# Order of the k, q and V loads and casts in an attention and SwiGLU kernel

## The chip, the cores and the metric

The kernel runs on one core of one Trainium2 chip. The metric is the device time of one execution in microseconds. The mean granted TensorE clock counts half clock only after full clock has come for the first time: the 0.991 of the kernel before is its 6.83 us of half clock from 76.9 us on in 401.1 us, without the first 12.0 us. The engines are called TensorE, VectorE, ScalarE, GpSimd and SyncE; in profile lines they are PE (PEld for its weight loads), DVE, ACT, POOL and SP. A "q" behind a name is the engine's instruction queue.

## The reference, cut to what matters

```python
# 8 batches x 8 heads, 576 positions, head size 64
scores = 0.125 * q @ k.T + minimum(bias, 0)      # bias from a cumulative sum of max(s, 0)
scores[causal] = -1e9                            # above the diagonal
attn = softmax(scores)
x = (attn @ v)        # heads side by side: 4608 x 512
out = (silu(x @ w_gate) * (x @ w_val)) @ w_out   # 512 -> 1536 -> 512
```

## The kernel before

The program works on half-batches of four heads (16 of them). Heads 0 to 7 (batch 0) come first. After that the feed-forward stage of one block of 512 rows is interleaved with the attention of the next batch: a generator yields items of feed-forward work, and another yields pieces of attention. What this Python emits first for an engine comes first in that engine's timeline: in the kernel before V 1 had landed by 55.0 us, but its casts on GpSimd, emitted behind those of k, q 4, began at 59.57.

The k, q of a half-batch ("k, q 3" are those of half-batch 3, "V 1" is the V of batch 1) take this way: a load to SBUF in fp32, a cast to bf16, and a transposition. For half-batches 0 to 4 TensorE transposes them; from 5 on they go through a scratch in DRAM and are transposed by a DMA on the way back. V is loaded per batch in five pieces into one buffer, and from batch 1 on each piece is cast on GpSimd.

```python
raw = ctx.enter_context(tc.tile_pool(name="raw", bufs=3))        # k, q: three buffers each
...
loaded["v", b] = raw.tile([128, NCH, H, D], FP32, tag="rawv", bufs=1, name="rawv")   # V: one buffer
...
# first batch, h = head 0..7
if h == 3:
    aug(2, SP4)          # four small DMAs of bias rows, issued by SyncE
    load_qk(3)
if h == 7:
    aug(3, SP4)
    load_v(1, range(5))
    load_qk(4)
    cast_one(2, "k", nc.gpsimd)
    cast_one(2, "q", nc.gpsimd)
    w_load("o", 0)
    w_load("o", 1)
...
# attention from head 8 on: kk is the head, h the half-batch, step the head in it
if step == 3 and h + 2 < NPE:            # NPE = 5; only h = 2: casts of half-batch 4
    cast_one(h + 2, "k", nc.gpsimd)
    cast_one(h + 2, "q", nc.gpsimd)
...
for ci in range(4):
    score_piece(kk, ci)                  # matmuls, exp on ScalarE, causal mask on GpSimd
    if ci == 1:
        side(h, step)                    # loads and casts ahead; casts of V 1 at head 11
...
PREP_AT = {                              # where TensorE transposes half-batch h + 1
    2: {(1, 3): 0, (2, 1): 1, (2, 3): 2, (3, 1): 3},
    3: {(0, 3): 0, (1, 3): 1, (2, 1): 2, (2, 3): 3},
}
...
hook = {                                 # at the n-th item of the first feed-forward block
    ...
    9: [lambda: cast_one(3, "k", nc.gpsimd), lambda: cast_one(3, "q", nc.gpsimd)],
    21: [lambda: load_qk(5)],
}
```

In `side`, the load of k, q `h + 3` is issued at the first head of half-batch h, from h = 3 on (so half-batch 6 at head 12), and V 2 is loaded at heads 10 and 11.

The softmax here doesn't subtract the row's maximum and nothing guards it: scores larger than these inputs give would overflow.

Of the kernel before, what the change touches and what calls it, by code (L numbers as in the profile page):

```python
# [19 lines left out]
def kernel(  # L20
# [11 lines left out]
    nc = tc.nc  # L32
# [48 lines left out]
    NPE = 5  # L81
# [24 lines left out]
    with tc.manual_schedule():  # L106
# [41 lines left out]
        def load_one(hb, name, rs=(0, NR)):  # L148
            b, g = divmod(hb, 2)
            if rs[0] == 0:  # L150
                loaded[name, hb] = raw.tile([128, NR, J, D], FP32, tag="raw" + name, name="raw" + name)
            nc.sync.dma_start(  # L152
                loaded[name, hb][:, rs[0] : rs[1], :, :].rearrange("x r j d -> x r (j d)"),
                SRC[name][0][b, g * HB + 2 * rs[0] : g * HB + 2 * rs[1], :, :].rearrange(
                    "(r e) (p j) d -> (e p) r (j d)", e=2, j=J
                ),
            )

        def load_qk(hb):
            load_one(hb, "k")  # L160
            load_one(hb, "q")

        def load_v(b, cs):
            if 0 in cs:
                loaded["v", b] = raw.tile([128, NCH, H, D], FP32, tag="rawv", bufs=1, name="rawv")
            t = loaded["v", b]
            for c in cs:
                n = 128 if c < 4 else TAIL
                nc.sync.dma_start(  # L169
                    t[0:n, c, :, :],  # L170
                    v[b, :, c * 128 : c * 128 + n, :].rearrange("h p d -> p h d"),
                )
# [12 lines left out]
        def aug(hb, engs):  # L185
            for hh in range(HB):
                r, e = divmod(hh, 2)
                r0 = 64 * (1 - r)
                bh = hb * HB + hh
                engs[hh].dma_start(  # L190
                    KQ[hb % 2][r][r0 : r0 + 4, :, e * S : (e + 1) * S],
                    HL[bh : bh + 1, :, :, :],
                )
# [48 lines left out]
        def cast_one(hb, name, eng):  # L242
            cts[name, hb] = cp.tile([128, J, NR, D], BF16, tag="c" + name, bufs=2, name="c" + name)
            dst = cts[name, hb].rearrange("x j r d -> x r j d")
            src_t = loaded[name, hb]
            if eng is nc.scalar:
                nc.scalar.copy(dst, src_t)
            else:
                eng.tensor_copy(dst, src_t)  # L249
# [75 lines left out]
        def w_load(kind, j, h=None):  # L325
            dst = {"g": WG, "v": WV, "o": WO}[kind][j]
            if kind == "o":
                src_ap = moe_w_out[j * WKO * 128 : (j + 1) * WKO * 128, :].rearrange(
                    "(c p) n -> p c n", p=128
                )  # L330
            else:
                w = moe_w_gate if kind == "g" else moe_w_val
                lo, hi = (0, WCH) if h is None else (h * WCH // 2, (h + 1) * WCH // 2)
                src_ap = w[:, j * WCH + lo : j * WCH + hi].rearrange("(c p) n -> p c n", p=128)
                dst = dst[:, :, lo:hi]
            nc.gpsimd.dma_start(dst, src_ap)
# [101 lines left out]
        def x_out(pr):  # L438
            nc.sync.dma_start(
                XS[pr].rearrange("(c p) d -> p c d", p=128), ots.pop(pr)  # L440
            )
# [6 lines left out]
        def x_pe(pr, eng=None):  # L448
            b, r = divmod(pr, H // 2)
            ot = ots.pop(pr)  # L450
            bs = take()
            ps = view16(bs, S)
            for c in range(NCH):
                n = 128 if c < 4 else TAIL
                nc.tensor.transpose(
                    ps[:, c * 128 : c * 128 + n], ot[0:n, c, :], ident[0:n, 0:n]
                )
            for lo, hi, at in x_parts(b):
                if eng is nc.scalar:
                    nc.scalar.copy(XT[:, r, at : at + hi - lo], ps[:, lo:hi])  # L460
                else:
                    nc.vector.tensor_copy(XT[:, r, at : at + hi - lo], ps[:, lo:hi])
            give(bs)
# [40 lines left out]
        def prep_one(hb, i):  # L504
            g, nm = divmod(i, 2)
            nm = ("k", "q")[nm]
            pe_transpose(hb, nm, g)
            for r in range(2):
                pe_out(hb, nm, g, r, nc.scalar if nm == "k" else nc.vector)

        PREP_AT = {
            2: {(1, 3): 0, (2, 1): 1, (2, 3): 2, (3, 1): 3},
            3: {(0, 3): 0, (1, 3): 1, (2, 1): 2, (2, 3): 3},
        }

        AV_AT = {
# [5 lines left out]
        def attn_items():  # L522
            for kk in range(H, BH + 2):
                h, step = divmod(kk, HB)
                if kk < BH:
                    if step == 3 and h + 2 < NPE:
                        cast_one(h + 2, "k", nc.gpsimd)
                        cast_one(h + 2, "q", nc.gpsimd)
                    if step == 0 and 3 < h + 1 < NPE:
                        aug(h + 1, GP4)  # L530
                    for ci in range(4):
                        score_piece(kk, ci)
                        if ci == 1:
                            side(h, step)
                        yield kk + 0.1 + ci / 8
                        if (step, ci) in PREP_AT.get(h, ()):
                            prep_one(h + 1, PREP_AT[h][step, ci])
                            yield kk + 0.1 + ci / 8
                for x in X_AT.get(kk, (kk - 2,)):
                    if x % 2 == 1 and H <= x < BH:  # L540
                        if x < XB * H:
                            x_pe(x // 2)
                            yield kk + 0.5
                        else:
                            x_in(x // 2)
                for p in AV_AT.get(kk, (kk - 1,)):
                    if H <= p < BH:
                        av_piece(p, (0, 1, 2))
                        yield kk + 0.6
                        av_piece(p, (3,))  # L550
                        yield kk + 0.7
                        av_piece(p, (4,))
                        av_out(p)
                        if p >= XB * H and p % 2 == 1:
                            x_out(p // 2)
                        yield kk + 0.8
# [103 lines left out]
        def first_batch():  # L660
            wq = {1: (("g", 0), ("v", 0)), 4: (("g", 1),), 5: (("v", 1),)}
            tail = {
                6: ("a0", "a1"),
                7: ("a2", "a3", "a4", "x0", "a5", "x1", "a6", "a7", "x2", "w6", "x3", "w8"),
            }
            for h in range(H):
                for ci in range(4):
                    score_piece(h, ci)
                for w in wq.get(h, ()):
                    w_load(*w)  # L670
                if h == 1:
                    order = [(nm, g) for g in range(2) for nm in ("k", "q")]
                    for nm, g in order:
                        pe_transpose(1, nm, g)
                    for r in range(2):
                        for nm, g in order:
                            pe_out(1, nm, g, r, nc.vector)
                    for c in range(3, 5):
                        cast_v(0, c, nc.vector)
                if h == 2:  # L680
                    for c in range(3):
                        cast_v(0, c, nc.gpsimd)
                if h == 3:
                    aug(2, SP4)
                    load_qk(3)
                if h == 7:
                    aug(3, SP4)
                    load_v(1, range(5))
                    load_qk(4)
                    cast_one(2, "k", nc.gpsimd)  # L690
                    cast_one(2, "q", nc.gpsimd)
                    w_load("o", 0)
                    w_load("o", 1)
                for what in tail.get(h, ()):
                    i = int(what[1:])
                    if what[0] == "a":
                        av_piece(i, range(NCH))
                        av_out(i)
                    elif what[0] == "x":
                        x_pe(i, nc.scalar)  # L700
                    else:
                        keep_warm(i)
# [6 lines left out]
        def pump(upto):  # L709
# [9 lines left out]
            2: [lambda: prep_one(2, 1)],  # L719
            3: [lambda: prep_one(2, 2)],  # L720
            4: [lambda: prep_one(2, 3)],
            9: [lambda: cast_one(3, "k", nc.gpsimd), lambda: cast_one(3, "q", nc.gpsimd)],
            21: [lambda: load_qk(5)],
        }
        for tt in range(NTT):
            lo = H * (tt + 1) + LAGS[tt]
# [40 lines left out]
```

## Time and profile before

| | kernel before |
|---|---|
| time, median of 4 | 403.07 us (401.6 to 405.39) |
| span of the profiled run | 401.1 us, mean clock 0.991 |
| TensorE busy | 370.0 us (92%) |
| idle of TensorE in gaps over 0.6 us, 30 to 380 us | 2.52 + 2.11 + 1.98 + 4.18 + 1.63 us |
| half clock | until 12.0 us, and 76.9 to 83.7 us |

The page has these two rows, with 40 slices of 10 us each. The first is the share of a slice in which TensorE was busy, in tenths, and the second the clock that it was granted, in tenths of full speed.

```profile
PE   3687959599999899999999999999999999999996
...
PEclk9999999889999999999999999999999999999999
```

From the ninth slice on TensorE is full, but for one 8 and the end. The two 8s of the clock row are the eighth and the ninth slice.

### The profile page before, as it was taken

The page shows a single profiled execution, that of the slowest core. Times are in us where ns is not written, and L with a number is a line of the kernel's source. Part 1 is how long each engine was busy: PE and PEld are TensorE (multiplying, and loading weights), DVE is VectorE, ACT ScalarE, POOL GpSimd, SP SyncE. Part 2 cuts the span into 40 slices and gives each one's busy share as a digit, 9 for nine tenths or more (in the row PEclk, how much of TensorE's full clock was granted, in tenths as well). Part 3 has the DMA queues.
Part 4 walks back from the last instruction along what each step waited for, and adds up shares of the span by engine and source line. Part 5 has one row for each costly group of instructions (what it writes and reads, how often), then busy time and mean ns, then how long its engine had stood idle before and what let it go on. Part 6 is the DMA issues. An engine that isn't in the chain of part 4 may idle for free.

```text
span 401.1 us, 7862 instructions
## 1 busy us (share of the span) xinstructions
PE 370.0 (92%) x2943; PEld 205.5 (51%) x2994; DVE 236.4 (59%) x431; ACT 214.1 (53%) x411; POOL 149.6 (37%) x270
## 2 busy tenths in 40 slices
PE   3687959599999899999999999999999999999996
PEld 3574535355555455555555555555555554444442
DVE  7865766316782287627952785479527743752750
ACT  7874963346665365555655565556556532323321
POOL 7780436454646173536453645364411100000000
PEclk9999999889999999999999999999999999999999
DMA  7999975693977697999688958794441014002002
GB/s 249 206 278 209 198 192 126 263 281 97 233 176 205 158 290 184 232 231 261 138 199 209 244 126 218 186 234 129 96 131 24 20 27 136 2 26 78 2 0 105
DMA packets 116982, 64.18 MB, mean 160 GB/s; under 512 B 97248, under 2 KB 101184, under 8 KB 116944
## 3 DMA queue, kind: packets, MB, share of 16 engines
q1 hardware_dynamic: 111456, 58.34, 57.1%
q0 software_dynamic: 5344, 5.21, 7.4%
q8 instruction: 23, 0.38, 0.4%
q10 hardware_dynamic: 144, 0.13, 0.1%
q14 instruction: 15, 0.12, 0.1%
HBM read 37.90 MB, written 19.86 MB: 144 GB/s over the span
## 4 chain that ended last, share of the span: by engine, by line
PE 76%; SPq 8%; DMA 7%; ACT 3%; DVE 2%; POOL 2%; issue 1%; POOLq 0%; ACTq 0%; DVEq 0%
PE bank L599 22%; PE bank L571 19%; PE bank L586 19%; PE bank L367 8%; SPq L169 7%; PE bank L405 6%; DMA rawk<-in_k_dram 2%; DMA pk<-ks 2%; DMA out_dram<-ysb 2%; PE wide L367 2%; ACT pt L380 1%; DMA rawq<-in_q_dram 1%; POOL vt L176 1%; SPq L152 1%; DVE ot L422 1%
## 5 line engine op out<-in xcount | busy, mean ns | idle before, releaser
L380 ACT ACTIVATE pt<-bank 128x512 bf16<-128x512 f32 x224 | 104.4, 506 | 49.1 <-PE bank L367 38.1
L578 DVE SCALAR_TENSOR_TENSOR pp<-th,bank 128x512 bf16<-128x512 bf16 x108 | 74.2, 687 | 80.4 <-ACT th L576 79.7
L586 PE MATMUL bank<-XT,wv 128*128 128x512 bf16 x421 | 109.4, 380 | 3.0 <-DMA wv<-in_moe_w_val_dram 2.5
L571 PE MATMUL bank<-XT,wg 128*128 128x512 bf16 x409 | 109.6, 380 | 1.7 <-DVE pp L578 0.2
L576 ACT ACTIVATE th<-bank 128x512 bf16<-128x512 f32 x108 | 64.5, 597 | 80.0 <-PE bank L571 76.0
L599 PE MATMUL bank<-wo,ht 128*128 128x512 bf16 x415 | 103.6, 384 | 1.0 <-issue 0.2
L383 POOL TENSOR_SCALAR_AFFINE_SELECT pt<-pt 128x512 bf16<-128x512 bf16 x64 | 40.9, 639 | 113.0 <-ACT pt L380 113.0
L591 DVE TENSOR_TENSOR ht<-pp,bank 128x512 bf16<-128x512 bf16 x108 | 74.0, 686 | 11.8 <-PE bank L586 3.1
L367 PE MATMUL bank<-kq 128*128 128x128 bf16 (+4 forms) x504 | 66.6, 242 | 4.0 <-DMA rawv<-in_v_dram 2.1
L367 PEld LDWEIGHTS <-kq 128*128 128x128 bf16 x576 | 46.5, 99 | 42.2 <-issue 7.0
L586 PEld LDWEIGHTS <-wv 128*128 128x128 bf16 x432 | 38.4, 98 | 37.0 <-DMA wv<-in_moe_w_val_dram 2.7
L599 PEld LDWEIGHTS <-ht 128*128 128x128 bf16 x432 | 38.7, 99 | 36.4 <-issue 1.1
L571 PEld LDWEIGHTS <-wg 128*128 128x128 bf16 x432 | 38.3, 98 | 36.6 <-issue 1.0
L405 PEld LDWEIGHTS <-pt 128*128 128x128 bf16 x960 | 41.8, 98 | 28.3 <-POOL pt L388 4.3
L405 PE MATMUL bank<-vt,pt 128*128 128x65 bf16 x840 | 43.4, 194 | 7.3 <-POOL pt L388 4.2
L616 ACT ACTIVATE ysb<-bank 128x512 f32<-128x512 f32 x35 | 20.9, 597 | 46.0 <-PE bank L599 38.6
L421 DVE RECIPROCAL rc<-bank 128x5 f32<-128x5 f32 x56 | 10.6, 190 | 38.4 <-PE bank L405 38.3
L388 POOL TENSOR_SCALAR_AFFINE_SELECT pt<-pt 128x64 bf16<-128x64 bf16 x64 | 16.1, 252 | 40.5 <-ACT pt L380 40.2
L190 POOL DMA_DIRECT2D kq<-HL x52 | 30.5, 587 | 1.0
L422 DVE TENSOR_TENSOR ot<-bank,rc 128x320 bf16<-128x320 f32 x56 | 27.5, 492 | 1.9
L176 POOL CAST vt<-rawv 128x512 bf16<-128x512 f32 (+1 forms) x38 | 22.5, 621 | 0.0
L249 POOL CAST ck<-rawk 128x1152 bf16<-128x1152 f32 x14 | 16.0, 1142 | 16.2 <-DMA rawk<-in_k_dram 16.2
(64 smaller groups left out, 161.8 us busy)
## 6 DMA issues: line engine op xcount, KB each, us to landing
out_dram<-ysb SPq DMA_DIRECT2D x35, 256.0 KB, 2.6
rawk<-in_k_dram SPq DMA_DIRECT2D x15, 576.0 KB, 10.2
rawq<-in_q_dram SPq DMA_DIRECT2D x15, 576.0 KB, 6.9
rawv<-in_v_dram SPq DMA_DIRECT2D x32, 256.0 KB, 4.8
xs<-ot SPq DMA_DIRECT2D x24, 160.0 KB, 2.5
ks<-ck SPq DMA_DIRECT2D x11, 288.0 KB
qs<-cq SPq DMA_DIRECT2D x11, 288.0 KB, 3.7
wg<-in_moe_w_gate_dram POOLq DMA_DIRECT2D x2, 768.0 KB, 14.8
```

The lines of the kernel that those rows point to most:

```text
L190: engs[hh].dma_start(KQ[hb % 2][r][r0 : r0 + 4, :, e * S : (e + 1) * S], HL[bh : bh + 1, :, :, :],)
L367: nc.tensor.matmul(sc[:, o : o + w], T[:, 1, e * S + 128 * tj : e * S + 128 * (tj + 1)], T[:, 0, e * S + lo : e * S + hi], start=True, sto ...
L380: nc.scalar.activation(pt[:, c0 : c0 + W], sc[:, 0:W], AF.Exp, scale=0.125)
L383: nc.gpsimd.affine_select(pt[:, 1088:1600], pt[:, 1088:1600], pattern=[[0, 4], [1, 128]], compare_op=ALU.is_ge, fill=zreg, base=0, channel ...
L405: nc.tensor.matmul(av[:, bi * (D + 1) : (bi + 1) * (D + 1)], pt[:, c0 : c0 + 128], VT[b % 2][:, tj, h, :], start=(tj == 0), stop=(tj == bi),)
L422: nc.vector.tensor_mul(ot[:, :, e * D : (e + 1) * D], av3[:, :, 0:D], rc[:, :, None].to_broadcast([128, NCH, D]),)
L571: nc.tensor.matmul(pg, WG[j][:, c, f0 : f0 + 128], xt[:, c, :], start=(c == 0), stop=(c == 3),)
L576: nc.scalar.activation(th, pg, AF.Tanh, scale=0.5)
L578: nc.vector.scalar_tensor_tensor(pp, in0=th, scalar=1.0, in1=pg, op0=ALU.add, op1=ALU.mult)
L586: nc.tensor.matmul(pv, WV[j][:, c, f0 : f0 + 128], xt[:, c, :], start=(c == 0), stop=(c == 3),)
L591: nc.vector.tensor_mul(ht, pp, pv)
L599: nc.tensor.matmul(py, hts[ft][:, ts_ * 128 : (ts_ + 1) * 128], WO[ft // WKO][:, ft % WKO, :], start=(ft == 0), stop=(ft == NFT - 1),)
```

## The change

Its intent is that no engine should stand at an operand whose load has been issued too late. k, q 5 go in front of V 2, k, q 3 behind their bias rows, the casts of half-batch 4 behind those of V 1, and the transposes of half-batch 3 come earlier. The change is also described as having the scratch writes of x and the output stores on SyncE; they are there in both kernels.

```diff
         PREP_AT = {
-            2: {(1, 3): 0, (2, 1): 1, (2, 3): 2, (3, 1): 3},
-            3: {(0, 3): 0, (1, 3): 1, (2, 1): 2, (2, 3): 3},
+            2: {(0, 3): 0, (1, 3): 1, (2, 1): 2, (2, 3): 3},
+            3: {(1, 3): 0, (2, 1): 1, (2, 3): 2, (3, 1): 3},
         }
...
-                    if step == 3 and h + 2 < NPE:
-                        cast_one(h + 2, "k", nc.gpsimd)
-                        cast_one(h + 2, "q", nc.gpsimd)
+                    if step == 1 and 3 < h + 1 < NPE:
+                        cast_one(h + 1, "k", nc.gpsimd)
+                        cast_one(h + 1, "q", nc.gpsimd)
...
                 if h == 3:
                     aug(2, SP4)
-                    load_qk(3)
                 if h == 7:
                     aug(3, SP4)
+                    load_qk(3)
                     load_v(1, range(5))
                     load_qk(4)
                     cast_one(2, "k", nc.gpsimd)
                     cast_one(2, "q", nc.gpsimd)
+                    load_qk(5)
...
-            9: [lambda: cast_one(3, "k", nc.gpsimd), lambda: cast_one(3, "q", nc.gpsimd)],
-            21: [lambda: load_qk(5)],
+            6: [lambda: cast_one(3, "k", nc.gpsimd), lambda: cast_one(3, "q", nc.gpsimd)],
```

## The prediction

> **What bounds the kernel now.** I read the page first. TensorE is busy 370.0 of 401.1 us, and its row of the 40 slices is at 9 from the ninth slice on; the loss lies in the first 84 us. I then asked for the gaps of TensorE there in the timeline.
>
> ```profile
> 33.86 1.04 PE L586 MATMUL bank<-XT,wv 128*128 128x512 bf16 x4 [2.52 <-DMA wv<-in_moe_w_val_dram]
> ...
> 54.54 0.38 PE L367 MATMUL bank<-kq 128*128 128x128 bf16 x4 [2.11 <-DMA rawv<-in_v_dram]
> ...
> 60.23 0.22 PE L405 MATMUL bank<-vt,pt 128*128 128x65 bf16 x2 [1.98 <-POOL vt L176]
> ...
> 78.11 0.35 PE L405 MATMUL bank<-vt,pt 128*128 128x65 bf16 x3 [4.18 <-POOL pt L388]
> ```
>
> The columns are start, duration, engine, line, and in brackets the idle time before and its releaser. There are four gaps: 2.52 us, 2.11 us, one from 58.2 to 62.4 us that holds 1.1 us of work (so about 3.1 us idle), and 4.18 us. Two of the releasers are GpSimd, so its timeline is next.
>
> ```profile
> 56.44 1.14 POOL L249 CAST ck<-rawk 128x1152 bf16<-128x1152 f32 x1 [6.89 <-DMA rawk<-in_k_dram]
> 57.89 1.15 POOL L249 CAST cq<-rawq 128x1152 bf16<-128x1152 f32 x1 [0.31 <-DMA rawq<-in_q_dram]
> 58.99 0.64 POOL L383 TENSOR_SCALAR_AFFINE_SELECT pt<-pt 128x512 bf16<-128x512 bf16 x1
> 59.57 2.83 POOL L176 CAST vt<-rawv 128x512 bf16<-128x512 f32 x5
> ...
> 75.61 1.14 POOL L249 CAST ck<-rawk 128x1152 bf16<-128x1152 f32 x1 [9.27 <-DMA rawk<-in_k_dram]
> 76.70 1.17 POOL L176 CAST vt<-rawv 128x512 bf16<-128x512 f32 x2
> 77.82 0.24 POOL L388 TENSOR_SCALAR_AFFINE_SELECT pt<-pt 128x64 bf16<-128x64 bf16 x1
> ```
>
> Twice GpSimd stands at a cast whose data has not landed, and what TensorE needs queues behind it: first the casts of V 1 behind those of half-batch 4, then the small mask of head 13 behind the cast of k 5. The SyncE queue shows when those loads were issued.
>
> ```profile
> 27.26 23.66 SPq L169 DMA_DIRECT2D rawv<-in_v_dram  x5
> 50.97 1.69 SPq L152 DMA_DIRECT2D rawk<-in_k_dram  x1
> ...
> 62.43 5.57 SPq L169 DMA_DIRECT2D rawv<-in_v_dram  x5
> 68.04 0.62 SPq L152 DMA_DIRECT2D rawk<-in_k_dram  x1
> ...
> 69.22 0.47 SPq L152 DMA_DIRECT2D rawk<-in_k_dram  x1
> ```
>
> These are V 1 (23.66 us to issue), k 4, V 2, k 6 and k 5; k 3 had been issued at 19.2 us, in front of them. The instruction list of the built kernel has half-batch 6 in front of 5, because the load of 5 hangs on item 21 of the feed-forward stage. V 2 cannot be issued before V 1 is cast, as they share one buffer. Hence the chain: k, q 4 late, V 1 cast late, V 2 late, k 5 later still. Last, the stretches around the fourth gap (length; then busy time of TensorE, weight loads, VectorE, ScalarE, GpSimd; granted clock):
>
> ```profile
> 75.00:80.00 5.00, 1.66 (x10) 1.05 (x12) 0.69 (x2) 0.60 (x1) 4.39 (x7) 0.69 0.42 158
> 80.00:85.00 5.00, 5.00 (x35) 2.56 (x34) 1.03 (x3) 1.80 (x4) 2.42 (x6) 0.63 0.87 261
> ```
>
> The gap also costs clock. The clock records have half speed from 76.9 to 83.7 us; TensorE works in it from 78.1, so it loses half of 5.6 us, 2.8 us.
>
> [...] the 4.18 us gap is followed by half clock, the gaps of 2.1 and 2.5 us are not. [...] V 1 had landed by 55.0 us (the SyncE queue, which had to see it before V 2, was then released) and its casts began at 59.57. [...] V has 256-byte packets, and V 0 was issued in 4.11 us without the weights beside it, V 1 in 23.66 us with them.
>
> **The change part by part.** The scratch writes of x and the output stores named with the change are on SyncE in both kernels; the diff does not touch them, so they count zero. No work is added or removed: every engine has the same number of instructions. What moves:
>
> *Load of k, q 3 behind the bias rows of half-batch 3.* It is issued near 25.7 us in place of 19.2: the last of those four small loads reuses the completion semaphore of q 2, and the queue passed that wait at 25.0 us before. The weights have the DMA engines alone for about 3.2 us. Weight packets took 0.134 us per engine (packet records), 24 in that time against some 15 beside k, q: nine packets, 1.2 us earlier for the weights that the 2.52 us gap waits for. Gain 1.2 us, an estimate. k, q 3 then land near 34 us, V 1 as before near 55, since the bytes in front of its end are the same.
>
> *Casts and transposes of half-batch 3 earlier* (the casts hang on item 6 of the feed-forward stage, not 9; each block of transposes comes half a head to one head sooner). The 2.11 us gap is named for a V load, but that is a coincidence: the weight load there waits for VectorE too, whose copy of q 3 (53.69, first of two of about 0.7 us) ends at 54.42, and TensorE goes on at 54.54. In the new order three groups of four feed-forward matmuls (0.86 us each) and a whole head's scores stand between the last transposes and that use. Gain 2.1 us.
>
> *Casts of half-batch 4 behind V 1.* TensorE reaches the first use of V 1 at 58.2 - 1.2 - 2.1 - 0.4 (a transpose block of half-batch 4 moved behind it) = 54.5 us. GpSimd casts each piece of V as it lands, the last by 55.0 + 0.6 = 55.6. Ideal passage is 54.5 + 1.1 = 55.6, against 62.4 now. So 62.4 - 55.7 = 6.7 us have been won by then, of which about 3.1 here.
>
> *k, q 5 in front of V 2 and 6.* k, q 4 landed at 56.3 and 57.7; the next 1.18 MB at about 400 GB/s (measured 373 in 70 to 75 us) take 3 us, so k, q 5 land near 61. GpSimd needs k 5 only after bias rows 4 (2.4 us), two masks (0.9), the casts of 4 (2.3) and one more mask: at 62. The 4.18 us gap goes, and the 2.8 us of half clock with it. Gain 7.0 us.
>
> *Cost.* That same row on GpSimd makes cast k 4 end at about 55.7 + 0.2 + 2.4 + 0.9 + 1.1 = 60.3, while TensorE comes to its transposes at about 55.7 + 3.8 = 59.5 (66.25 - 62.4 is the 3.8). A new wait of 0.8 us. The displaced transpose block gives back 0.4.
>
> Sum: 1.2 + 2.1 + 3.1 + 7.0 + 0.4 - 0.4 - 0.8 = 12.6 us; I take 12, so 403 - 12 = 391. After 84 us TensorE is full and its order hardly differs, so the shift should reach the end.
>
> **Rivals.** *The loads stay the bound.* From 20 to 57 us the DMA engines are nearly always busy; if V 1 lands late (k, q 3 now start in front of it later), TensorE waits at the first V product. For: TensorE arrives within 1 us of the last piece. Against: V 1 keeps its place among the bytes. Each us later costs one[...]. *GpSimd becomes the bound* as its backlog of 9 us after V 1 is now set against a TensorE that is 7 us ahead. For: the 0.8 us above. Against: the mask of head 13 is ready near 65, needed near 68. If it is 3 us worse: 394. *The gain is given back later* on the way of half-batch 5 through its scratch in DRAM. For: its use moves 12 us forward. Against: its casts and stores move forward as much (cast of q 5 from 78.6 to about 66), and V 2 is issued at 56 instead of 62. If half of the shift is lost: 397. *Nothing moves* because the wait was hidden anyway: against it, all four gaps are on TensorE itself.
>
> **Range and chances.** The gaps are measured and sum to 14.7 us with the clock, a floor of about 388. Landing times are good to perhaps 2 us, and one rival coming half true costs 3 to 5. Range 388 to 395.5. 2% is 394.96, which only a rival passes: 0.86 for faster, 0.13 for within, 0.01 for slower.
>
> **What would show it.** Right: no TensorE gap of over 2 us from 34 to 84 us, granted clock 1.0 in 75 to 85, V 1 casts ended by 56 to 57 with those of half-batch 4 behind, cast of k 5 near 62 without a wait for its load, and TensorE 12 us ahead at the end of its first output stage. Wrong: a GpSimd wait for V 1 past 57, half clock anywhere from 50 to 90, or a new TensorE gap at the scores of half-batch 4 or 5.

## More of the kernel before

All runs but two were in the fast state, with a mean granted TensorE clock between 0.98 and 1.00. The two slow ones, one of the kernel before (405.48 us, clock 0.981) and one of the kernel called both (396.9 us), are left out of the ratios.

## The result, and the profile after

The kernel after took 391.06 us in the median of 4 runs (388.98 to 392.82), against 403.07 before. The ratio is 0.9695, with a 95% interval of 0.9628 to 0.9761. A ratio here is the mean time of one kernel's fast runs over that of the other's in the same rounds, so it is not quite the ratio of the medians that are quoted. The kernel after was run once more later as a control, in five rounds: 390.66 us, ratio 0.9701 (0.9649 to 0.9754). Both intervals lie under 0.98, so the kernel is faster by more than 2%.

The predicted time was 391.0 us. The two rows of the page of the kernel after, whose slices are 9.8 us each:

```profile
PE   3789999999999889999999999999999999999996
...
PEclk9969999999999999999999999999999999999999
```

The dents of the sixth and eighth slice are gone, and so is the half clock near 80 us. A new stretch of half clock lies in the third slice, in the first heads. It is not in every run: the control's profile has a mean clock of 0.999 and no such stretch, and its span is 388.2 us against 391.1.

From 34 to 100 us the timeline of TensorE has no gap over 0.25 us. Two later ones of over 1 us are left (start, duration, engine, line; in brackets the idle time before and its releaser):

```profile
128.09 0.38 PE L367 MATMUL bank<-kq 128*128 128x320 bf16 x2 [1.32 <-ACT ysb L616]
...
145.42 1.02 PE L571 MATMUL bank<-XT,wg 128*128 128x512 bf16 x4 [1.66 <-DVE pp L578]
```

The first was there before as well, at 139.5 us with 1.63 us. The second was 0.24 us before. On GpSimd, the casts on which the argument rests:

```profile
52.43 3.03 POOL L176 CAST vt<-rawv 128x512 bf16<-128x512 f32 x5
...
58.76 1.14 POOL L249 CAST ck<-rawk 128x1152 bf16<-128x1152 f32 x1
59.84 1.14 POOL L249 CAST cq<-rawq 128x1152 bf16<-128x1152 f32 x1
...
61.53 1.13 POOL L249 CAST ck<-rawk 128x1152 bf16<-128x1152 f32 x1
```

V 1 is cast 7 us earlier, then comes half-batch 4, then k 5, and none of these lines has a wait in brackets. On the SyncE queue, V 1 takes about as long to issue as before (22.83 us against 23.66), k, q 4 and 5 follow at once, and V 2 comes 7 us earlier:

```profile
28.66 22.83 SPq L169 DMA_DIRECT2D rawv<-in_v_dram  x5
51.53 0.62 SPq L152 DMA_DIRECT2D rawk<-in_k_dram  x1
...
52.76 0.41 SPq L152 DMA_DIRECT2D rawk<-in_k_dram  x1
...
55.49 9.10 SPq L169 DMA_DIRECT2D rawv<-in_v_dram  x5
```

To see where the time was won, I compare the start of the same instruction in three profiles. The control has no half clock except at its start and end, so it shows the order of the work with least luck in it.

| start of (us) | before | after | control | before minus control |
|---|---|---|---|---|
| first tanh of the feed-forward stage | 31.14 | 33.91 | 32.66 | -1.5 |
| second tanh | 36.08 | 36.15 | 34.89 | 1.2 |
| reciprocal behind the second V product of batch 1 | 64.36 | 59.99 | 58.73 | 5.6 |
| first output rows on ScalarE | 72.56 | 67.29 | 66.03 | 6.5 |
| first tanh of the second block | 93.04 | 81.95 | 80.69 | 12.4 |
| first tanh of the third block | 139.45 | 128.04 | 126.98 | 12.5 |
| first tanh of the fourth block | 179.06 | 169.08 | 166.13 | 12.9 |
| end | 401.1 | 391.1 | 388.2 | 12.9 |

All of the gain is there by 81 us, and it holds to the end. In the first profile of the kernel after it shrinks from 11.4 to 10.0 us between the third and the fourth block, where the 1.66 us gap is.

The start is 1.5 to 2.8 us later than before, and that goes with the clock rather than with the change. The clock records give the moment at which full clock first came: 12.0 us before (matmuls of 128 columns start 107 ns apart in front of it and 55 behind it) and 15.2 in the control. Of the experiments below, the one with the old load of k, q 3 in the kernel after (not_hb3) had full clock from 16.0 us and its first tanh at 32.98. Two with parts of the change in the kernel before had full clock from 11.4 (only_cast4) and 16.4 us (only_hb3), and the first tanh at 30.86 and 32.58. In the first profile of the kernel after full clock came at 12.8, but half clock followed from 19.6 to 26.5 us.

### The profile page after: what moved, and what is told of

It reads as the page before. It is cut to its first block, busy times and chain, and to the rows that moved or that the text cites.

```text
span 391.1 us, 7867 instructions
## 1 busy us (share of the span) xinstructions
PE 369.5 (94%) x2944; PEld 205.9 (53%) x2994; DVE 235.5 (60%) x431; ACT 214.2 (55%) x411; POOL 149.8 (38%) x270
## 3 DMA queue, kind: packets, MB, share of 16 engines
q1 hardware_dynamic: 111456, 58.34, 60.6%
## 4 chain that ended last, share of the span: by engine, by line
PE 84%; DVE 5%; DMA 5%; ACT 3%; issue 1%; SPq 0%; DVEq 0%; ACTq 0%
PE bank L599 23%; PE bank L571 21%; PE bank L586 21%; PE bank L367 9%; PE bank L405 6%; DMA pk<-ks 2%; PE wide L367 2%; ACT pt L380 2%; DMA out_dram<-ysb 1%; DVE pp L578 1%; PE one L405 1%; DVE kq L320 1%; DMA kq<-HL 1%; DVE ht L591 1%; DMA s_sb<-in_s_dram 1%
## 5 line engine op out<-in xcount | busy, mean ns | idle before, releaser
L616 ACT ACTIVATE ysb<-bank 128x512 f32<-128x512 f32 x35 | 20.9, 597 | 45.0 <-PE bank L599 36.5
L278 DVE COPY kq<-pk 64x1152 bf16<-64x1152 bf16 x22 | 13.2, 599 | 8.0 <-DMA pk<-ks 7.9
```

## The experiments

The change has three parts that can be done or undone alone: k, q 5 in front of V 2 and k, q 6; everything on half-batch 3; and the casts and transposes of half-batch 4. The theory is that the four gaps are links of one chain, so that a part is worth what the next link lets through. The rival is that each part is worth its own gap. Seven kernels test this and one idea about the clock. Four more, with the control among them, look for a better kernel. All gave correct results. They ran in three groups on three chips, each with its own runs of the kernel before (medians 402.89, 401.32 and 403.01 us), so ratios are compared rather than times.

### k, q 5 alone, on the kernel before (only_kq5)

```diff
                     cast_one(2, "q", nc.gpsimd)
+                    load_qk(5)
...
-            21: [lambda: load_qk(5)],
```

> Kernel before, with the load of k, q 5 alone moved in front of V 2 and of k, q 6. Chain theory (each TensorE gap is one link of a chain of loads and GpSimd casts): V 1 is still cast behind half-batch 4, so TensorE passes the first V product at about 62.4 us as before; then GpSimd casts k 5 without a wait near 66 us, the 4.18 us gap and the half clock after it (2.8 us) go: 396 us, 7 less. Rival (moving k, q 5 forward only makes V 2 late by as much, and the stall moves to the casts of V 2): within 2 us of before, with a GpSimd wait for a V load of 3 us or more at 66 to 72 us.

Measured: 397.6 us (395.8 to 399.25), ratio 0.988 (0.9818 to 0.9942). GpSimd, in its timeline, casts k 5 without a wait and then the pieces of V 2, with 0.18 us of waiting before the second:

```profile
67.54 1.14 POOL L249 CAST ck<-rawk 128x1152 bf16<-128x1152 f32 x1
68.62 0.61 POOL L176 CAST vt<-rawv 128x512 bf16<-128x512 f32 x1
69.41 0.62 POOL L176 CAST vt<-rawv 128x512 bf16<-128x512 f32 x1 [0.18 <-DMA rawv<-in_v_dram]
```

The fourth gap is gone, so the rival, a stall moved to V 2, falls. The gain is 1.2% or 4.8 us where 7 were expected, which the interval still holds. In this profile the clock accounts for the shortfall: it has half clock from 55.1 to 58.5, from 61.9 to 65.3 and from 137.0 to 140.4 us, 10.2 us in all, against 6.8 before. The first of these follows a gap of 2.12 us; behind the 2.52 us gap of the kernel before there was none. From the second V product to the second block 6.6 us were won, as expected, and 2.3 us were lost just in front, where the half clock fell. But this profile is of the slowest run; the others had clocks of 0.994 to 0.996, and for them a shortfall is not explained.

### Half-batch 3 alone, on the kernel before (only_hb3)

```diff
-            2: {(1, 3): 0, (2, 1): 1, (2, 3): 2, (3, 1): 3},
+            2: {(0, 3): 0, (1, 3): 1, (2, 1): 2, (2, 3): 3},
...
                     aug(2, SP4)
-                    load_qk(3)
...
                     aug(3, SP4)
+                    load_qk(3)
...
-            9: [lambda: cast_one(3, "k", nc.gpsimd), lambda: cast_one(3, "q", nc.gpsimd)],
+            6: [lambda: cast_one(3, "k", nc.gpsimd), lambda: cast_one(3, "q", nc.gpsimd)],
```

> Kernel before, with only the part on half-batch 3: its load behind its bias rows, its casts at item 6, its transposes earlier. Chain theory: the gaps of 2.5 and 2.1 us close, but TensorE then waits at the first V product, whose time (62.4 us) is set by the landing of k, q 4 and the casts behind it; so the time is that of before within 1 us, 403, with a gap or several of 7 to 8 us in all near 54 to 62 us and half clock after it; the next gap takes up what the half clock costs. Rival (the gaps add up, as the sum of the prediction treats them): 3 to 4.6 us less, 399.

Measured: 402.47 us (401.37 to 405.74), ratio 1.0015 (0.9947 to 1.0084). This is the clearest of the runs. TensorE's timeline:

```profile
58.15 0.45 PE L291 MATMUL bank<-ident,ck 128*128 128x128 bf16 x5 [2.50 <-POOL ck L249]
60.70 0.24 PE L405 MATMUL bank<-vt,pt 128*128 128x65 bf16 x2 [2.09 <-POOL vt L176]
...
78.56 0.27 PE L405 MATMUL bank<-vt,pt 128*128 128x65 bf16 x3 [1.40 <-POOL pt L388]
```

The gaps of 2.52 and 2.11 us have gone, and nothing is won. TensorE waits instead at the transposes of half-batch 4 and at V 1. Half clock follows, from 60.8 to 67.6 us, and slows the stretch behind. The fourth gap shrinks from 4.18 to 1.40 us, but it ends at the same moment as before (78.56 against 78.11), because the landing of k 5 ends it: its cast starts at 76.05 us, 75.61 before. The waits came to some 5 us, not 7 to 8; the time came out as the chain had it. The rival's 399 us lie outside the interval.

### The casts of half-batch 4 alone, on the kernel before (only_cast4)

```diff
-            3: {(0, 3): 0, (1, 3): 1, (2, 1): 2, (2, 3): 3},
+            3: {(1, 3): 0, (2, 1): 1, (2, 3): 2, (3, 1): 3},
...
-                    if step == 3 and h + 2 < NPE:            # casts h + 2
+                    if step == 1 and 3 < h + 1 < NPE:        # casts h + 1
```

> Kernel before, with only the casts of half-batch 4 behind V 1 (and its transposes later). Chain theory: TensorE passes the first V product near 58.9 us in place of 62.4; V 2 can then be issued 7 us earlier, so k 5, still behind V 2 and k, q 6, lands near 69 us in place of 75.5, and the 4.18 us gap shrinks to about 1 us, without half clock: 3.5 + 3 + 2.8, some 9 us less, 394. Rival (each part is worth its own gap only): 3.1 us less, 400, with the fourth gap still 4 us and the half clock still there.

Measured: 396.64 us (396.27 to 398.97), ratio 0.9873 (0.9803 to 0.9943). First TensorE's timeline, then that of GpSimd:

```profile
54.32 0.38 PE L367 MATMUL bank<-kq 128*128 128x128 bf16 x4 [2.11 <-DVE kq L320]
...
72.58 0.27 PE L405 MATMUL bank<-vt,pt 128*128 128x65 bf16 x3 [2.19 <-POOL pt L388]
```

```profile
70.08 1.14 POOL L249 CAST ck<-rawk 128x1152 bf16<-128x1152 f32 x1 [7.81 <-DMA rawk<-in_k_dram]
```

The part moves V 1, and with it V 2 and k 5: the cast of k 5 starts at 70.1 us in place of 75.6, and the fourth gap halves. That is the chain. It was oversized: k 5 came 1 us later than I had it, the gap kept 2.19 us instead of about 1, and half clock followed it all the same, for 3.4 us. So the gain is some 5 us, between the 9 of the theory and the 3.1 of the rival. By time alone the rival's 400 us is just inside the interval and the theory's 394 outside; what refutes the rival is the trace, since its fourth gap would have stayed at 4 us.

The first line also names the true releaser of the 2.11 us gap. The same gap of the same length is here put down to VectorE's copy of q 3, as the prediction had argued against the name in the profile of the kernel before. The semaphore records settle it. The bias rows of half-batch 3 and the last piece of V 1 count on one semaphore. In the kernel before, that piece was still landing (54.14 to 55.00 us) when TensorE went on at 54.54; here its counts came from 54.87 us on, when TensorE had already gone on.

### The kernel after without k, q 5 (not_kq5), without the casts of 4 (not_cast4), without half-batch 3 (not_hb3)

Each takes back one of the three diffs above from the kernel after.

> Kernel after, with the load of k, q 5 put back to its old place behind V 2 and k, q 6. Chain theory: V 1 is cast by 55.5 us as in the kernel after, V 2 is issued at once, k 5 lands near 68 us and the small mask of head 13 is done near 71, where TensorE needs it near 67.5: a gap of about 3 us, half clock in perhaps half of the runs; 394.5 us (393 to 397). Rival (k, q 5 carries its 7 us whatever the rest does): 398.

Measured: 395.45 us (393.06 to 398.18), ratio 0.9848 (0.9778 to 0.9918), within the range of the chain theory. TensorE, then GpSimd:

```profile
72.36 0.35 PE L405 MATMUL bank<-vt,pt 128*128 128x65 bf16 x3 [3.70 <-POOL pt L388]
```

```profile
69.86 1.14 POOL L249 CAST ck<-rawk 128x1152 bf16<-128x1152 f32 x1 [7.61 <-DMA rawk<-in_k_dram]
```

A gap of 3.70 us is back, with half clock from 71.0 to 77.8 us, in the slowest of the four runs. k 5 still comes 6 us earlier than in the kernel before. The cost is 1.5 points against the control, some 5.9 us, between the 3.5 of the theory and the 7 of the rival; the rival's 398 us lies inside the interval too. So the run shows the gap and its cause, and not which size is right.

> Kernel after, with the casts of half-batch 4 put back in front of those of V 1 (and its transposes to their old place). Chain theory: TensorE comes to the first V product near 54 us and passes it near 62.4, 6.7 us later than in the kernel after, and half clock follows the wait, 2.6 us; no later gap: 398.5 us (397 to 400.5). Rival (only its own gap of 3.1 us returns): 394.

Measured: 397.04 us (396.08 to 397.88), ratio 0.9885 (0.9832 to 0.9938): 1.8 points behind the control, some 7.4 us. The casts of V 1 start at 59.5 us as in the kernel before. TensorE, then GpSimd:

```profile
60.15 0.22 PE L405 MATMUL bank<-vt,pt 128*128 128x65 bf16 x2 [2.14 <-POOL vt L176]
```

```profile
59.48 2.84 POOL L176 CAST vt<-rawv 128x512 bf16<-128x512 f32 x5
```

TensorE waits there, half clock follows from 60.3 to 63.7 us, and no later gap is over 1.2 us. The rival, 394 us, lies outside the interval. A part whose own gap was 3.1 us costs more than twice that when it is taken out. In this profile 5.4 us are lost from the second tanh to the second V product (29.2 us against 23.8 in the control): 3.7 us of waits, and the rest fits the 3.4 us at half clock. What is beyond that is not located; half clock from 19.4 to 26.2 us, in the first heads, has its share, and the mean clocks of the four runs (0.983 to 0.991) are lower than those of the control.

> Kernel after, with the part on half-batch 3 put back (load in front of its bias rows, casts at item 9, transposes later). Chain theory: the gaps of 2.5 and 2.1 us return, and nothing later waits any more, so they now cost what they last less what TensorE still waits at the first V product: it passes there near 58.9 us instead of 55.7; 394 us (392.5 to 396). Rival (this part is worth nothing, as alone): 391.

Measured: 391.64 us (390.9 to 393.47), ratio 0.9758 (0.9703 to 0.9813). That is under the theory's range of 392.5 to 396 and close to the rival. By the ratio it is 0.6 points behind the control, some 2.3 us, but the two intervals overlap, and neither 394 nor 391 is excluded: this experiment decides nothing on the time. The 2.11 us gap is back:

```profile
54.14 0.38 PE L367 MATMUL bank<-kq 128*128 128x128 bf16 x4 [2.11 <-DMA rawv<-in_v_dram]
```

The 2.52 us gap is not: TensorE began the feed-forward stage 1.8 us later than in the kernel before and waited 0.30 us for the weights.

Together: alone, the three parts give 1.2, -0.2 and 1.3%, 2.3% in sum, and all three give 3.0%. Taken out singly, they cost 1.5, 0.6 and 1.8 points, 3.9 in sum. With errors of about 0.7 points on each ratio these sums do not differ for certain, from each other or from 3.0. That a part is not worth its own gap rests on only_hb3, whose interval excludes the rival and whose waits return at the next gates, and on the fourth gap, which the traces of only_cast4 and only_hb3 show halved or cut to a third by parts that do not touch it. not_cast4 excludes its rival too, but more by half clock than by waits.

### A warm TensorE in the first heads (warm)

```diff
                 for w in wq.get(h, ()):
                     w_load(*w)
+                if h >= 2:
+                    keep_warm(6)      # six 128x128 matmuls of the identity, no result used
```

> Kernel after, with six matmuls of the identity (no result used) after the scores of heads 2 to 7, where TensorE waits for ScalarE. Theory on the clock: the kernel after loses about 2 us [...] (granted clock 0.99 in the profile), and the run with clock 1.0 took 389.0; [...] clock 1.0 from 12 to 385 us in the profile, 389.0 us and a narrower spread. Rival (the spread of the runs has another cause, or the added matmuls stand in the way of the scores): 391 or more, with the spread as before.

Measured: 394.35 us (391.43 to 394.83), ratio 0.9794 (0.9725 to 0.9864). The idea, work for TensorE where it waits in heads 2 to 7, failed. The profile has full clock from 16.6 us on through the first heads, but so has that of the control, from 15.2 us on, without the added matmuls; that they did anything for the clock is not shown. The first tanh came at 34.27 us, later than in any other run: full clock came late, and the added matmuls wait for a buffer just in front of a head's scores (1.41 us at 18.55). Then a gap of 2.44 us at 146.0, the place of the 1.66 us gap in the kernel after, was followed by half clock from 146.3 to 149.8. One run had a mean clock of 1.000 and still took 394.47 us. So neither the first heads nor the counted half clock is all of it.

### The control, and the gaps that are left (after_again, y4, kq_behind, both)

```diff
-    yp = ctx.enter_context(tc.tile_pool(name="yp", bufs=3))       # y4, both
+    yp = ctx.enter_context(tc.tile_pool(name="yp", bufs=4))
```

```diff
-            if h >= 3 and h + 3 < NHB and step == 0:               # kq_behind, both
-                load_qk(h + 3)
             if h + 1 < NHB and h + 1 >= NPE:
                 if step == 0:
                     transposes(h + 1)
                     aug(h + 1, GP4)
                 ...
+            if h >= 3 and h + 3 < NHB and step == 0:
+                load_qk(h + 3)
```

> The kernel after unchanged, as the control of this group: ratio to before near 0.97, 391 us, with single runs between 388.5 and 393 according to where half clock falls [...].

> Kernel after with four buffers for the output rows in place of three. Theory: the gap of 1.3 us at 128 us is ScalarE waiting for the landing of an output store that SyncE issued late; a fourth buffer takes it away: 389.7 us, 1.3 less than the control. Rival (the gap only moves to the wait for the transposed k at 145 us, which is set by the landing): same as the control within 0.5 us, with a gap of 2.5 us or more near 145 us.

> Kernel after with each later load of k, q put behind the transposes from scratch on the SyncE queue, where it stood in front of them. Theory: the 7.5 us from issue to use of the transposed k of that stage hold some 3 us of k, q packets in front of it; without them the 1.7 us gap at 145 us goes, and the half clock that follows it in some runs: 389 us, 1.5 to 2.5 less than the control. Rival (the transposes are slow by themselves, and the loads held back behind their wait come late): control or up to 2 us more.

> Both of these edits on the kernel after. Theory: the two gaps, 1.3 and 1.7 us, go together: 388 us, 3 less than the control. Rival (only one of the two counts): 389.5.

| kernel, 6 runs each | median us | ratio to before (95%) | mean clocks of the runs |
|---|---|---|---|
| control (kernel after) | 390.66 | 0.9701 (0.9649 to 0.9754) | 0.991 to 1.000 |
| y4 | 395.5 | 0.9805 (0.9765 to 0.9845) | 0.985 to 0.991 |
| kq_behind | 394.45 | 0.9782 (0.9736 to 0.9827) | 0.981 to 1.000 |
| both | 392.85 | 0.9736 (0.9683 to 0.979) | 0.994 to 1.000 |

The run of both at 396.9 us, which was slow, is in its median and not in its ratio. None of the edits wins, and the times of kq_behind and both lie above what theory and rival had said. In y4 the gap near 128 us is gone, and TensorE starts the third block at 123.3 us in place of 127.0. It then stands at the next gate. First TensorE's timeline of y4, then VectorE's:

```profile
147.06 1.87 PE L571 MATMUL bank<-XT,wg 128*128 128x512 bf16 x4 [6.74 <-DVE pp L578]
```

```profile
145.37 0.92 DVE L278 COPY kq<-pk 64x1152 bf16<-64x1152 bf16 x2 [8.52 <-DMA pk<-ks]
```

VectorE stands for 8.52 us at its copies of the transposed k, and its feed-forward work, emitted behind them, goes on at 146.32 us. TensorE idles for 6.74 us, and half clock follows for 6.8 us, which the last 1.87 us for four matmuls shows (1.02 at full clock). This is the rival of y4, and worse than it was written. Part of it stays open: SyncE issued this transpose at 135.64 us, and 9.7 us went by until the copy, where the same transpose took 6.1 us in the control and 7.6 in the first profile of the kernel after. The load of k, q that SyncE had issued just in front of it had its last packet at 142.3 us, against 139.1 and 141.7. Why that load took longer is not known.

In kq_behind the transposed k does come sooner: from issue to VectorE's copy the middle nine of eleven have a median of 5.8 us (5.5 in both), against 6.5 in the control. This suggests that packets of k, q in front were part of that delay, but the first profile of the kernel after has 7.6, so two profiles of one kernel differ by more. But the gap near 128 us stays, the transposes of x are now issued behind and cost 1.16 us at 123.9, and ScalarE waits for an output store at 253 us:

```profile
252.98 1.02 PE L586 MATMUL bank<-XT,wv 128*128 128x512 bf16 x4 [2.28 <-ACT ysb L616]
```

Half clock follows from 253.9 to 260.7 us. Both edits together are nearer to the control, but not better. The kernel after has the lowest ratio of those tried.

## Why the prediction was right

By its own steps, with the control's profile where half clock would blur the reading:

- **Loads of k, q 3 later, weights earlier.** The direction was right, the size too small. The weights of the gap had their last packet at 28.67 us against 32.03, so 3.4 us earlier and not 1.2, and the gap of 2.52 us closed wholly. From the first to the second tanh 2.23 us went by, against 4.94: 2.7 us won. The prediction gave the weights 3.2 us without packets of k, q beside them; in the control there were none for 9.0 us (20.9 to 29.9). What I had not foreseen is that the stage began 1.5 us later, by the clock of the start.
- **Half-batch 3 earlier.** Right: the 2.11 us gap is gone, and only_cast4 shows that it belonged to VectorE's copy.
- **Casts of half-batch 4 behind V 1.** The cast of V 1 was put to end at 55.6 us; it ended at 55.5 in both profiles. TensorE came to the first product of V 1 at 56.8 us (55.6 in the control), not at 54.5, and had no wait. The gain by then is 5.6 us in the control; the prediction had 6.7.
- **k, q 5.** Right: cast of k 5 at 61.5 us without a wait for its load (predicted near 62), gap and half clock gone. Between the second V product and the second block 6.8 us were won (5.6 to 12.4); the prediction had 7.0 less a cost of 0.8.
- **Cost of 0.8 us at the transposes of half-batch 4.** It did not come. The cast of k 4 ended at 59.9 us, as it was put (60.3), but TensorE arrived there at 61.9 us (60.6 in the control) and not at 59.5.
- **The shift reaches the end.** Nearly: 12.9 us in the control. In the first profile 1.4 us were given back at the gap of 1.66 us, by VectorE's wait for the transposed k. That is the rival "given back later" in a small size, and later than where I had looked for it.

So the sum of 12.6 us, taken as 12, stands against 12.9 us between the spans of the profile before and the control, and against 12.0 us between the medians. The errors of the terms are 0.6 to 1.5 us each, and they cancel: the mechanism was right, but that the total is right to half a microsecond is luck. Two slips did not matter: 2% below 403.07 is 395.0 us, not 394.96, and the copy of q 3 ended at 54.39, not 54.42.

The clock is a larger share of the medians than of the one profile that the prediction used. In the control's rounds the runs of the kernel before had mean clocks of 0.982 to 0.991, 0.987 in the mean of 11, and those of the control 0.9975 in the mean of 6. The difference of 0.0106 times 400 us is at most 4.2 us, if TensorE was busy throughout the half clock. The prediction had 2.8. It also counted on half clock behind the gap of 4.18 us alone, from one profile, in which the gaps of 2.1 and 2.5 us had none behind them; in the later runs half clock followed gaps of 2.12 us (only_kq5) and 2.44 us (warm).

Shown by runs: that half-batch 3 alone gives nothing, that the cast of V 1 behind half-batch 4 costs some 7 us in the kernel after, and that k 5 in its old place brings the fourth gap back. Only argued: how much of each time is half clock, since its stretches fall differently in each run, and what half-batch 3 is worth in the kernel after.

## What to carry to other kernels

Where work for the busiest engine queues behind an instruction that waits, as here the mask of head 13 behind GpSimd's 9.27 us of waiting for k 5, ask of each instruction in that queue whether its operand has landed by the time the queue gets there, and put the ones that land late behind the ones that are needed soon. Gaps that hang on one chain of loads are not to be summed: find the gate that is set by something absolute, such as a landing, since closing a gap in front of it only lengthens the wait at it (half-batch 3 alone: 4.6 us of gaps closed, nothing won). A gap can cost more than its length: with the one of 4.18 us came 6.83 us of half clock, 2.8 us of work by the estimate in the prediction. And removing a harmless one can open a larger one at the next gate (y4: the 1.52 us gap of the control gone, one of 6.74 us opened).

## What the traces show of the clock, the queues and the releasers

- Half clock lasted 6.83 us in the kernel before (from 76.88 us) and in the kernel after (from 19.64), and 3.4 us in only_kq5 (55.1 to 58.5). The gap with it differs: half clock began at 55.08 us in only_kq5 after a gap of 2.12 us (52.3 to 54.4), and at 76.88 us in the kernel before, in the gap of 4.18 us, while the gaps of 2.52 us in the kernel before and of 1.52 us in the control were followed by none. In the kernel after it came back from 19.64 to 26.47 us, where no gap was over 0.9 us. What idle time brings it on is not shown by these runs.
- Full clock first came between 11.4 us (only_cast4) and 16.6 us (warm) in the profiles, and the first tanh between 30.9 and 33.0 us in the ten without half clock or added matmuls in the first heads, which is 0.5% of the kernel.
- In the kernel before V 0 took 4.11 us to issue with no weights beside it (no weight packet from 10.9 to 15.0 us), V 1, of the same size, 23.66 us with them (1,410 weight packets from 27.3 to 51.0 us). From 37 to 41 us 434 weight packets of 1,536 bytes went beside 457 of V's 256 bytes.
- The name of a releaser can be a coincidence: the same gap of 2.11 or 2.12 us was put down to a V load in three profiles (the kernel before, only_kq5, not_hb3) and to VectorE's copy in a fourth (only_cast4).
